# Three small copies of v off the DMA queue, and one clear moved, in a sliding-window attention with an MLP behind it

## The chip, the cores and the metric

The kernel runs on one core of one Trainium2 chip. A core has a matrix engine (TensorE, PE in the profile), VectorE (DVE), ScalarE (ACT), GpSimd (POOL) and SyncE (SP), each with its own queue of instructions, worked off in order, and sixteen DMA engines. DMAs are issued from SyncE's and GpSimd's queues here. The metric is the device time of one execution in microseconds (us).

## The reference

Attention with a causal window of 64 over 8 batches of 8 heads, 576 rows and 64 dimensions, and an MLP over the 4608 rows that come out, with the gate h * cos(h):

```python
scores = scale * np.matmul(q, k.transpose(0, 1, 3, 2))
rel = pos[:, None] - pos[None, :]
mask = (rel >= 0) & (rel < window)          # window = 64
scores = np.where(mask, scores, -1000000000.0)
attn = np.exp(scores - np.max(scores, axis=-1, keepdims=True))
attn = attn / (np.sum(attn, axis=-1, keepdims=True) + 1e-09)
x = np.matmul(attn, v)                      # then (B, S, H * D) -> 4608 x 512
h = x @ w_in                                # w_in 512 x 2048
g = h * np.cos(h)
out = g @ w_out                             # w_out 2048 x 512
```

## The kernel before

The MLP goes in nine tiles of 512 rows. Two heads make a pair; a unit is (batch b, pair p, block j) of 64 query rows, with 128 keys and both heads of the pair on the 128 partitions. Units are worked in groups of three or four. A group n goes through these steps:

- scores on TensorE (`s`, `Gs`), then mask and maximum on VectorE (`m`, `Gm`), the exponentials on ScalarE (`e`, `Ge`, L318), the reciprocal of their sums on VectorE (`i`, `Gi`, L325),
- the product of both, on GpSimd or VectorE (`n`, `Gn`, L332; the last letter names the engine, p for GpSimd, d for VectorE),
- the transpose of the product: for some groups on TensorE with a copy behind it (`w`, `Gw`, then `c`, `Gp`), for the others as a DMA transpose from SyncE's queue (`Gc`, L344).

Then come the values, that is weights times v, on TensorE (`v` for half of tile 0, `V` for pair p of tile 1), and a copy into xT (`x`, `X`). The MLP of a tile is `h` (first matrix), the sine on ScalarE (`S`), the gate on VectorE (`g`), `o` (second matrix) and `oc` (the copy of its result). An `h` takes one of five PSUM banks and needs the gate done that last used it.

v is loaded in chunks of 128 rows (`Lv0`, `Lv1` for batches 0 and 1) into every second slot of a tile of v. A unit whose keys begin in the middle of a chunk takes the slots between, which hold the neighbouring halves of two chunks. `spread_v` (L186 to L194) fills these slots with a copy from one slot into the next, by half of the partitions: as a DMA from SyncE's queue (letter s), on VectorE (d) or on GpSimd (p). Its steps are zA, zB and zC for batch 0 and y for batch 1; y.0 is the first half, y.1 the second. Both halves of a pair are needed before the values that use them: zB before v.0.1, y before V.0.

`ms.4` to `ms.7` clear the q blocks that batch 3 will use.

For tile 0 and the start of tile 1 the order of all instructions is written out by hand in the string FIRST: a step's place in it is its place in the queue of its engine. From there on a planner puts the attention of the next batches between the matrix products of a tile by due times (`at`, `pump`). For batch 2 it issues the transposes of k (`turn_k`, L247) and two copies of v on SyncE; for later batches the copies of v are on GpSimd.

The loads of weights, q, k and v go through GpSimd's queue: `Lwi` and `Lwo` for the four parts of w_in and w_out, `Lq` and `Lk` for q and k. 

Of the kernel before, what the change touches and what calls it, by code (L numbers as in the profile page):

```python
# [10 lines left out]
def _safe_warn(msg, *a, **kw):  # L11
# [58 lines left out]
)  # L70


# [1 line left out]
def kernel(  # L74
# [10 lines left out]
    B, H, S, D = q.shape  # L85
# [45 lines left out]
    def copy(engine, out, in_):  # L131
        {"a": nc.scalar.copy, "p": nc.gpsimd.tensor_copy}.get(engine, nc.vector.tensor_copy)(out, in_)  # L132
# [54 lines left out]
    def spread_v(b, half, engine="p", lo=0, hi=4):  # L187
        vt = vtiles[b % 2]
        hi = min(hi, 4 - (half == 0))
        d = slice(64 * half, 64 * half + 64)  # L190
        of = 2 * lo + 2 * (half == 0)
        to, of = vt[d, 2 * lo + 1:2 * hi:2], vt[d, of:of + 2 * (hi - lo) - 1:2]
        if engine == "s":
            nc.sync.dma_start(out=to, in_=of)  # L194
        else:
            copy(engine, to, of)
# [27 lines left out]
    def put_q(b, p, engine=None):  # L224
        of, to = in_order(st.pop(("tq", b, p)), qtiles[b * PAIRS + p], b)
        if b:
            copy(engine, to, of)
        elif engine == "a":
            nc.scalar.mul(to, of, scale)
        else:  # L230
            nc.vector.tensor_scalar(to, of, scale, None, ALU.mult)
# [17 lines left out]
    def put_k(b, p, engine="a"):  # L249
        kt = k_tile(b)[:, p]  # L250
        of, to = in_order(st.pop(("tk", b, p)), kt, b)
        copy(engine, to, of)
# [16 lines left out]
    def g_scores(n, which):  # L269
        s_ps = bank((BANKS if n < n_listed else S_BANKS)[which], "s_ps")  # L270
        units = groups[n]
        s_ps = s_ps[:, 0:len(units) * 128].rearrange("p (u c) -> p u c", c=128)
        if n < n_first:
            m0 = 2 if units[0][2] else 0
            for h in range(2):
                d = slice(64 * h, 64 * h + 64)
                nc.tensor.matmul(out=s_ps[d].rearrange("p u c -> p (u c)"), lhsT=ident[d, d],
                                 rhs=mask16[d, m0:m0 + len(units)].rearrange("p u c -> p (u c)"),
                                 start=True, stop=False, skip_group_check=True)
        for u, (b, p, j) in enumerate(units):  # L280
            kt = st["kT", b, p]
            lo = max(64 * j - 64, 0)
            rhs = kt[:, lo:lo + 128].rearrange("d (a t) -> d a t", a=2)
            if j and j % 2 == 0:
                rhs = rhs[:, ::-1, :]
            if b > 1:
                nc.tensor.matmul(out=s_ps[:, u].rearrange("p (a t) -> p a t", a=2),  # L287
                                 lhsT=qblocks[(b % 2) * PAIRS + p][:, j].rearrange("d h t -> d (h t)"), rhs=rhs,
                                 start=True, stop=True, skip_group_check=True)
                continue  # L290
            for h in range(2):
                d = slice(64 * h, 64 * h + 64)
                nc.tensor.matmul(out=s_ps[d, u].rearrange("p (a t) -> p a t", a=2),  # L293
                                 lhsT=qtiles[b * PAIRS + p][d, 64 * j:64 * j + 64], rhs=rhs[d], start=n >= n_first,
                                 stop=n >= n_first or u == len(units) - 1, skip_group_check=True)
        st["s", n] = s_ps


    def g_max(n):
        s_ps, units = st["s", n], groups[n]  # L300
        negm = att.tile([128, GF], F32, tag="negm", name="negm", bufs=8)
        if n < n_first:
            nc.vector.tensor_reduce(out=negm[:, 0:len(units)], in_=s_ps, op=ALU.max, axis=AX.X, negate=True)
        else:
            s = att.tile([128, GF, 128], F32, tag="s", name="s", bufs=4)
            for u, (b, p, j) in enumerate(units):
                nc.vector.tensor_tensor_reduce(out=s[:, u], in0=s_ps[:, u], in1=mask[:, 2 - j % 2 if j else 0],  # L307
                                               scale=-scale if b else -1.0, scalar=BIG, op0=ALU.add, op1=ALU.min,
                                               accum_out=negm[:, u:u + 1])
            st["s", n] = s  # L310
        st["m", n] = negm
# [152 lines left out]
    n = n_listed  # L464
# [45 lines left out]
    def spread_first(lo, hi):  # L510
        return lambda i, engine: spread_v(0, i, engine, lo, hi)
# [10 lines left out]
             "pq": lambda p, engine: put_q(0, p, engine), "pk": lambda p, engine: put_k(0, p, engine),  # L522
             "Pq": lambda p, engine: put_q(1, p, engine), "Pk": lambda p, engine: put_k(1, p, engine),
             "zA": spread_first(0, 1), "zB": spread_first(1, 3), "zC": lambda engine: spread_v(0, 1, engine, 3, 4),
             "y": lambda half_, engine: spread_v(1, half_, engine),
             "s": lambda p, g, which: g_scores(2 * p + g, which), "m": lambda p, g: g_max(2 * p + g),
             "e": lambda p, g: g_exp(2 * p + g), "i": lambda p, g: g_inv(2 * p + g),
# [12 lines left out]
    for mt in range(1, n_mt):  # L540
# [5 lines left out]
        for ff in range(n_ff):  # L546
# [8 lines left out]
            e = ff % 2  # L555
# [5 lines left out]
        for ms0 in range(0, MT // 128, 2):  # L561
            o_sb = moe.tile([128, 2, d_model], F32, tag="out", name="out_sb", bufs=OUTS)
            o_ps = [bank(which, "out_ps") for which in (("O1",) if mt == n_mt - 1 and ms0 else ("O1", "O0"))]
            for e in range(2):
                ms = ms0 + e
# [44 lines left out]
```

## Time and profile before

| | |
|---|---|
| median of 3 runs | 313.28 us (312.45 to 314.71) |
| the profiled execution | 313.61 us, span 311.8 us |
| granted TensorE clock | 1.0 |
| busy in the span | PE 95%, ACT 76%, DVE 74%, POOL 61% |
| the chain that ended last | PE 83%, DMA 8%, ACT 3%, POOL 3% |
| v copies by DMA in the first 60 us | issued at 17.35, 18.11, 19.49 and 47.60 us |
| tile 0 and the start of tile 1 | until about 64 us |

The span is the stretch between the first and the last instruction of one profiled execution; the time of the execution holds some 1.8 us more. The profile's views name instructions by engine, line, operation and tiles, with output before input. In views in order of time the first number is the start within the span and the second the duration, both in us; several instructions of a kind that follow each other are merged into one row (x3), and what stands in brackets is the idle time of the engine ahead of the row and what ended it. SPq is SyncE's queue of DMA issues: the duration there is that of issuing, and the data land later. PEld is TensorE's loading of weights.

### The profile page before, as it was taken

To read this page: it belongs to the slowest core of one execution; us is meant where nothing else is said; L and a number is where in the kernel's file an instruction comes from. 1 tells how busy PE (TensorE), PEld (TensorE's weight loads), DVE (VectorE), ACT (ScalarE), POOL (GpSimd) and SP (SyncE) were. 2 spreads that over 40 slices of the span, in tenths; PEclk is the share of its full clock that TensorE was granted. 3 is DMA by queue.
4 is the path that set the end of the run, shared out by engine and by line. 5 is a ranking of instruction groups with operands and counts; after the bars stand their busy time and mean duration, and the time that the engine had idled before them with its cause. 6 is when DMAs were issued, how large, how long until landed. Compare 5 with 4: busy or idle time off the path is not lost.

```text
span 311.8 us, 7954 instructions
## 1 busy us (share of the span) xinstructions
PE 296.8 (95%) x2627; PEld 161.6 (52%) x2659; DVE 230.6 (74%) x877; ACT 236.1 (76%) x785; POOL 191.7 (61%) x227
## 2 busy tenths in 40 slices
PE   3789999799999999999999999999999999999996
PEld 3667844445555455445545545455545554454443
DVE  5898978489777976798579867987698758335801
ACT  5998799486997799769976997699869986116600
POOL 8988576993569678966997699769902850000000
PEclk9999999999999999999999999999999999999999
DMA  7999999999959996999999998999794333011011
GB/s 150 175 212 187 200 178 132 132 162 167 241 82 113 138 235 84 117 116 230 120 105 129 216 138 94 139 230 120 91 135 155 65 80 141 0 69 68 0 67 70
DMA packets 155162, 41.17 MB, mean 132 GB/s; under 512 B 143280, under 2 KB 150384, under 8 KB 155120
## 3 DMA queue, kind: packets, MB, share of 16 engines
q0 software_dynamic: 100192, 18.06, 80.8%
q1 hardware_dynamic: 54784, 22.40, 38.1%
q8 instruction: 21, 0.34, 0.5%
q14 instruction: 21, 0.17, 0.2%
q10 hardware_dynamic: 144, 0.20, 0.2%
HBM read 36.70 MB, written 9.44 MB: 148 GB/s over the span
## 4 chain that ended last, share of the span: by engine, by line
PE 83%; DMA 8%; ACT 3%; POOL 3%; DVE 1%; issue 1%; SPq 1%; POOLq 0%; DVEq 0%; ACTq 0%
PE h_ps L428 34%; PE out_ps L570 34%; DMA w_in<-in_moe_w_in_dram 4%; PE s_ps L287 4%; PE h_ps L392 3%; PE o_ps L359 3%; ACT e L318 2%; PE tq_ps L214 2%; DMA wT<-w 2%; DMA k<-in_k_dram 2%; POOL v L183 1%; PE out_ps L440 1%; PE out_ps L411 1%; DVE s L307 1%; SPq L344 1%
## 5 line engine op out<-in xcount | busy, mean ns | idle before, releaser
L570 PE MATMUL out_ps<-w_out,gT 128*128 128x512 bf16 x482 | 116.1, 379 | 0.8 <-issue 0.2
L428 PE MATMUL h_ps<-xT,w_in 128*128 128x512 bf16 x498 | 115.2, 379 | 1.0
L556 ACT ACTIVATE sin<-h_ps 128x512 f32<-128x512 f32 x128 | 74.0, 598 | 34.0 <-PE h_ps L428 30.8
L318 ACT ACTIVATE e<-s,negm 128x128 f32<-128x128 f32 x256 | 98.7, 388 | 0.7 <-DVE negm L307 0.6
L559 DVE TENSOR_TENSOR gT<-h_ps,sin 128x512 bf16<-128x512 f32 x128 | 81.6, 685 | 21.4 <-ACT sin L556 20.6
L332 POOL TENSOR_TENSOR w<-e,rden 128x512 bf16<-128x512 f32 (+1 forms) x75 | 71.2, 965 | 38.7 <-DVE rden L325 36.9
L428 PEld LDWEIGHTS <-w_in 128*128 128x128 bf16 x512 | 48.6, 98 | 53.9 <-issue 0.4
L570 PEld LDWEIGHTS <-gT 128*128 128x128 bf16 x496 | 45.9, 98 | 44.2
L307 DVE CUSTOM_DVE_ANT_0 s<-s_ps,mask 128x128 f32<-128x128 f32 x256 | 58.5, 286 | 1.2 <-PE s_ps L293 1.0
L318 ACT ACTIVATION_READ_ACCUMULATOR e<-s,negm 128x1 f32 x256 | 48.1, 188 | 0.0
L177 POOL DMA_DIRECT2D q<-in_q_dram x36 | 29.0, 805 | 11.1 <-DMA v<-in_v_dram 4.3
L183 POOL DMA_DIRECT2D v<-in_v_dram x40 | 34.1, 873 | 0.4 <-DMA q<-in_q_dram 0.3
L177 POOL DMA_DIRECT2D k<-in_k_dram x36 | 28.8, 802 | 6.9 <-DMA k<-in_k_dram 5.6
L325 DVE RECIPROCAL rden<-den 128x4 f32<-128x4 f32 (+1 forms) x79 | 13.7, 173 | 21.0 <-ACT e L318 17.2
L132 ACT COPY out_sb<-out_ps 128x512 f32<-128x512 f32 (+1 forms) x18 | 10.2, 565 | 24.5 <-PE out_ps L570 18.4
L287 PEld LDWEIGHTS <-qB 128*128 128x128 bf16 x216 | 17.1, 98 | 14.2
L132 DVE CAST xT<-o_ps 128x512 bf16<-128x512 f32 x24 | 15.6, 677 | 10.8 <-PE o_ps L359 10.8
L132 DVE COPY out_sb<-out_ps 128x512 f32<-128x512 f32 x18 | 12.4, 689 | 13.5 <-PE out_ps L570 12.4
L132 DVE COPY qB<-tq_ps 64x576 bf16<-64x576 bf16 x48 | 21.6, 450 | 0.3
L287 PE MATMUL s_ps<-kT,qB 128*128 128x128 bf16 x216 | 21.9, 219 | 0.0
L307 DVE DVE_READ_ACCUMULATOR2_ANT negm<- 128x1 f32 x256 | 21.3, 83 | 0.0
L132 POOL COPY v<-v 64x1536 bf16<-64x1536 bf16 (+1 forms) x10 | 16.8, 1676 | 0.3
(64 smaller groups left out, 253.2 us busy)
## 6 DMA issues: line engine op xcount, KB each, us to landing
out_dram<-out_sb SPq DMA_DIRECT2D x16, 512.0 KB, 7.8
v<-in_v_dram POOLq DMA_DIRECT2D x32, 128.0 KB, 6.1
q<-in_q_dram POOLq DMA_DIRECT2D x36, 96.0 KB, 8.9
k<-in_k_dram POOLq DMA_DIRECT2D x36, 96.0 KB, 9.0
w_in<-in_moe_w_in_dram POOLq DMA_DIRECT2D x4, 512.0 KB, 9.2
w_out<-in_moe_w_out_dram POOLq DMA_DIRECT2D x4, 512.0 KB, 11.3
wT<-w SPq DMA_TRANSPOSE x68, 4.1
q<-in_q_dram POOLq DMA_DIRECT2D x7, 144.0 KB, 6.2
```

The costliest lines, as they stand in the source:

```text
L132: {"a": nc.scalar.copy, "p": nc.gpsimd.tensor_copy}.get(engine, nc.vector.tensor_copy)(out, in_)
L177: nc.gpsimd.dma_start(out=st[name, b][:, c].rearrange("p (h d) -> p h d", h=H), in_=src.rearrange("h p d -> p h d"))
L183: nc.gpsimd.dma_start(out=vt.rearrange("p (h d) -> p h d", h=H), in_=v[b, :, c * 128:c * 128 + n, :].rearrange("h p d -> p h d"))
L287: nc.tensor.matmul(out=s_ps[:, u].rearrange("p (a t) -> p a t", a=2), lhsT=qblocks[(b % 2) * PAIRS + p][:, j].rearrange("d h t -> d (h t)" ...
L307: nc.vector.tensor_tensor_reduce(out=s[:, u], in0=s_ps[:, u], in1=mask[:, 2 - j % 2 if j else 0], scale=-scale if b else -1.0, scalar=BIG, ...
L318: nc.scalar.activation(e[:, u], s[:, u], AF.Exp, bias=negm[:, u:u + 1], scale=1.0 if n < n_first else -1.0, accum_out=den[:, u:u + 1])
L325: nc.vector.reciprocal(out=rden[:, 0:len(groups[n])], in_=den[:, 0:len(groups[n])])
L332: (nc.gpsimd if engine == "p" else nc.vector).tensor_tensor(out=w[:, 0:u], in0=e[:, 0:u], op=ALU.mult, in1=rden[:, 0:u].unsqueeze(2).to_br ...
L428: nc.tensor.matmul(out=st["h", ff], lhsT=w_in_sb[:, ks, ff * 128:ff * 128 + 128], rhs=st["xT", mt][:, ks], start=start, stop=stop)
L556: nc.scalar.activation(sin, h_ps, AF.Sin, bias=math.pi / 2.0)
L559: nc.vector.tensor_tensor(out=gt[:, e], in0=h_ps, in1=sin, op=ALU.mult)
L570: nc.tensor.matmul(out=o_ps[e], lhsT=gT[ff // 2][:, ff % 2, ms * 128:ms * 128 + 128], rhs=w_out_sb[:, ff], start=ff == 0, stop=ff == n_ff - 1)
```

## The change

The DMAs zB.0.s and zB.1.s (64 partitions, two slots of 512) and zC.s (one slot) become copies on VectorE, each at a later place of FIRST than the DMA had: zB.0.d behind the maximum m.3.1, zB.1.d behind the copy c.0.1.d, zC.d behind the gate g.1.0. The clear ms.4.d moves from behind e.3.1 to behind g.0.3, ahead of ms.6. The DMA y.0.s (three slots) becomes two copies on GpSimd: yA.p (two slots) behind the product Gn.14.p, and yB.p (one slot) behind Gn.13.p. The copy y.1.d of the other half stays on VectorE. SyncE's queue has four DMAs fewer and nothing new; TensorE's and ScalarE's orders are the same.

The diff, cut to the lines of FIRST in which these steps stand:

```diff
-    "e.2.1 zB.0.s zB.1.s n.0.1.p i.1.1 w.3.0 v.0.0 c.3.0.d x.0.0.a s.3.1.3 Gm.10 v.1.0 m.3.1 i.2.1 "
-    "Gs.11.2 Gm.9 Gm.12 n.1.1.p x.1.0.a e.3.1 ms.4.d w.0.1 w.1.1 c.1.1.a i.3.1 h.0.0.1 h.0.1.4 tb "
-    "n.2.1.p c.0.1.d Lwi.3 w.2.1 h.0.2.0 n.3.1.p v.0.1 S.0.0 Gm.11 w.3.1 S.0.1 h.0.3.3 Lwo.0 S.0.2 "
-    "c.2.1.d c.3.1.d v.1.1 zC.s g.0.0 S.0.3 h.0.4.2 ms.5.d x.0.1.a x.1.1.d h.0.5.1 g.0.1 h.1.0.4 g.0.2 "
-    "g.0.3 S.0.4 ms.6.d h.0.6.0 h.1.1.3 S.0.5 S.1.0 Lq1.2 S.0.6 g.0.4 S.1.1 g.1.0 h.1.2.2 Lk1.2 ms.7.d "
...
-    "Gi.14 Gm.15 Gs.17.1 oc.1.d Gc.9 y.0.s Gn.11.p Gi.13 Gm.16 o.1.2 Ge.8 Ge.16 Ge.15 y.1.d Gn.14.p Gi.8 "
-    "Gc.12 Gm.17 o.0.3.0 Gi.16 Gn.13.p Gc.11 Gn.8.p Lq2.3 Lq2.4 Lq2.5 o.2.2 Gn.16.d Gw.8 Gc.14 Gc.13 "
...
+    "e.2.1 n.0.1.p i.1.1 w.3.0 v.0.0 c.3.0.d x.0.0.a s.3.1.3 Gm.10 v.1.0 m.3.1 zB.0.d i.2.1 Gs.11.2 Gm.9 "
+    "Gm.12 n.1.1.p x.1.0.a e.3.1 w.0.1 w.1.1 c.1.1.a i.3.1 h.0.0.1 h.0.1.4 tb n.2.1.p c.0.1.d zB.1.d "
+    "Lwi.3 w.2.1 h.0.2.0 n.3.1.p v.0.1 S.0.0 Gm.11 w.3.1 S.0.1 h.0.3.3 Lwo.0 S.0.2 c.2.1.d c.3.1.d v.1.1 "
+    "g.0.0 S.0.3 h.0.4.2 ms.5.d x.0.1.a x.1.1.d h.0.5.1 g.0.1 h.1.0.4 g.0.2 g.0.3 ms.4.d S.0.4 ms.6.d "
+    "h.0.6.0 h.1.1.3 S.0.5 S.1.0 Lq1.2 S.0.6 g.0.4 S.1.1 g.1.0 zC.d h.1.2.2 Lk1.2 ms.7.d Lq1.3 h.0.7.4 "
...
+    "Gs.17.1 oc.1.d Gc.9 Gn.11.p Gi.13 Gm.16 o.1.2 Ge.8 Ge.16 Ge.15 y.1.d Gn.14.p yA.p Gi.8 Gc.12 Gm.17 "
+    "o.0.3.0 Gi.16 Gn.13.p yB.p Gc.11 Gn.8.p Lq2.3 Lq2.4 Lq2.5 o.2.2 Gn.16.d Gw.8 Gc.14 Gc.13 Lk2.0 "
...
              "zA": spread_first(0, 1), "zB": spread_first(1, 3), "zC": lambda engine: spread_v(0, 1, engine, 3, 4),
+             "yA": lambda engine: spread_v(1, 0, engine, 0, 2), "yB": lambda engine: spread_v(1, 0, engine, 2, 3),
              "y": lambda half_, engine: spread_v(1, half_, engine),
```

16 rows, old and new, of the table FIRST are left out of this document.

## The prediction

> **What bounds the kernel now.** I read first the page's engine shares and the slices over the span, then the chain that ended last, then the order of time on SyncE, GpSimd and VectorE in the first 60 us.
>
> ```profile
> PE 296.8 (95%) x2627; PEld 161.6 (52%) x2659; DVE 230.6 (74%) x877; ACT 236.1 (76%) x785; POOL 191.7 (61%) x227
> PE   3789999799999999999999999999999999999996
> PE 83%; DMA 8%; ACT 3%; POOL 3%; DVE 1%; issue 1%; SPq 1%; POOLq 0%; DVEq 0%; ACTq 0%
> ```
>
> TensorE is busy 95% of the span, and from the second tile on (64 us) nearly without a gap: of 92 to 124 us it is busy 31.77 of 32.00. The change leaves TensorE's instructions and their order alone, so it can only move the date at which that steady part begins. What is to be won or lost lies in the first 64 us, where the chain leaves TensorE twice for a transfer. The second time is the one that matters (chain, start and us):
>
> ```profile
> 49.20 1.05 POOL w L332
> 50.25 0.59 SPq L344
> 50.93 1.21 SPq L344
> 52.22 5.68 DMA wT<-w
> 57.95 0.66 PE o_ps L359 x30
> ```
>
> Read backwards: at 57.95 TensorE starts V.2, the values of pair 2 in tile 1. It had finished V.1 at 56.49 and waited 1.46 us for the transposed weights of group 13 (step Gc.13). GpSimd had multiplied them by 50.24 (Gn.13), but SyncE issued their transpose only at 52.22, because its queue was late. Why it was late stands in SyncE's own order of time and in its waits:
>
> ```profile
> 43.78 2.58 SPq L344 DMA_TRANSPOSE wT<-w  x2
> 47.60 0.60 SPq L194 DMA_DIRECT2D v<-v  x1
> 48.30 3.83 SPq L344 DMA_TRANSPOSE wT<-w  x3
> SPq L194 <- DMA v<-in_v_dram: 16.8, 2, 15.7
> ```
>
> The two transposes Gc.10 and Gc.9 are out at 46.36. Then the queue stands before y.0.s, the copy of the first half of batch 1's v, until the loads of that v have landed (47.55); y.0.s takes its 0.60, and Gc.12, Gc.11 and Gc.14 follow at 48.30, 49.62 and 50.93, each 1.22 long, all of them on weights that had been ready (GpSimd ended Gn.12 at 45.52, Gn.11 at 46.52, Gn.14 at 48.21). Gc.13 comes behind them at 52.22.
>
> **The change, part by part.**
>
> *y.0.s off SyncE.* Gc.12 can go at 46.40, Gc.11 at 47.70, Gc.14 at 49.00 (three steps of 1.30), Gc.13 at 50.30, when Gn.13 has just ended. That is 1.9 us earlier. How long a transpose then takes to land is bounded by this tile's rows:
>
> ```profile
> DMA to landing us min/median/max: 3.8/5.5/6.7
> ```
>
> So the weights land between 54.1 and 57.0, with the median 55.8; I take the 5.69 of Gc.13 itself: 56.0, before V.1 ends. TensorE gains the whole 1.46 us; at the worst latency still 0.9.
>
> *yA and yB on GpSimd.* Here are the three multiplications between which they stand, and what GpSimd takes for such copies later in the run:
>
> ```profile
> 47.38 0.83 POOL L332 TENSOR_TENSOR w<-e,rden 128x384 bf16<-128x384 f32 x1 [0.86 <-PE s_ps L293]
> 49.20 1.04 POOL L332 TENSOR_TENSOR w<-e,rden 128x512 bf16<-128x512 f32 x1 [0.99 <-DVE rden L325]
> 51.14 1.04 POOL L332 TENSOR_TENSOR w<-e,rden 128x512 bf16<-128x512 f32 x1 [0.90 <-DVE rden L325]
> L132 POOL COPY v<-v 64x2048 bf16<-64x2048 bf16 x5 | 9.5, 1894 | 0.3
> L132 POOL COPY v<-v 64x1536 bf16<-64x1536 bf16 x5 | 7.3, 1458 | 0.0
> ```
>
> 512 columns more cost 436 ns, so yA (64x1024) is 1458 - 436 = 1.02 us and yB (64x512) 0.59. yA falls into the idle 0.99 before Gn.13, yB into the idle 0.90 before Gn.8: both are covered, to within 0.03. Without that cover Gn.13 would end up to 1.0 later; Gc.13 would then land by 57.0, and TensorE would still gain. Behind yB it is tighter, for Gn.8 is waited for: TensorE stood 0.59 us before Gw.8 at 52.23, and everything from there to V.2 follows without a gap.
>
> *Copies on VectorE and GpSimd at once.* The rows of the v copies that VectorE makes already:
>
> ```profile
> 17.56 0.25 DVE L132 COPY v<-v 64x512 bf16<-64x512 bf16 x1
> 18.57 0.34 DVE L132 COPY v<-v 64x512 bf16<-64x512 bf16 x1
> 49.69 1.09 DVE L132 COPY v<-v 64x2048 bf16<-64x2048 bf16 x1
> ```
>
> The first met an idle GpSimd, the other two a multiplication (until 18.76 and 50.24). If the last one waited out the 0.55 us that the multiplication still had, its own work was 0.55, and 512 columns cost about (0.55 - 0.25) / 3 = 0.10. By this reading y.1.d (49.69, in VectorE's queue ahead of Gi.8, which Gn.8 needs) and yB now meet. If the copy goes first, yB runs from 50.79 to 51.38, and Gn.8 starts 0.26 late; if yB goes first, Gi.8 is late by yB's 0.59. If the two engines do not block each other it costs nothing. Bounds 0 and 0.59; I take 0.3, near the first order, since the copy has been waiting by then. The Trainium skill speaks against the change here: by "SBUF — State Buffer", section "Who interferes with whom", a VectorE copy in a two-port mode and a GpSimd instruction take one port pair by turns, and the later of them is blocked until the other ends. By that rule this term is 0.26 to 0.59 and never 0; the three rows fit it.
>
> *zB on VectorE, ms.4 later.* zB.0.d and zB.1.d are 64x1024: 0.35 free, up to 1.4 if one waits for a whole multiplication of 1.04. zB.0.d (after m.3.1, at 21.03) finds GpSimd idle from 20.81; i.2.1, Gm.9 and Gm.12 behind it move by 0.3, and since ms.4 (0.45 from start to start) has left, i.3.1 is 0.2 early. zB.1.d then starts at 23.34, and n.3.1 on GpSimd at about 23.37: a tie. If VectorE is first, its delay is swallowed by its idle 0.67 us before c.3.1.d (25.45). If GpSimd is first, zB.1.d ends at 24.75. v.0.1, which now starts at 24.61 (right after the old zB.1.s landed, 24.55), would start at 24.8, c.3.1.d ends 0.4 later, and VectorE enters the gates 0.4 late.
>
> In the gates ms.4 and zC.d (0.25) come back into the queue, between g.0.3 and g.0.5: 0.7 us. Cover: TensorE takes 0.87 us for each h, VectorE 0.6 for each g, and h waits only for the g five banks back. h.1.3 (32.95) needs g.0.5, which now ends at 32.31: cover 0.64. With 0.7 and a VectorE that is 0.2 early TensorE waits hardly; with VectorE 0.4 late it waits some 0.4, and h.1.7 ends 0.55 late.
>
> *Three fewer transfers early.* zB.0.s, zB.1.s and zC.s (320 KB, issued from 17.35 on) share the sixteen DMA engines with the weight loads. At the rate of that stretch (about 200 GB/s) they are 1.6 us of transfer; I take 1.0 for the loads behind them. Two of these are waited for:
>
> ```profile
> 26.84 3.34 PE L392 MATMUL h_ps<-xT,w_in 128*128 128x256 bf16 x29 [0.18 <-DMA w_in<-in_moe_w_in_dram]
> 45.04 1.89 PE L411 MATMUL out_ps<-w_out,gT 128*128 128x512 bf16 x8 [0.30 <-DMA w_out<-in_moe_w_out_dram]
> ```
>
> The first wait, and the gap before v.0.1, give at most 0.45, which VectorE's gates then take back in part; the end of the gates lies between 0.2 early and 0.55 late, and I take 0.15 late. The second gives 0.3, whatever came before.
>
> **Sum.** Gates +0.15, w_out -0.3, yB +0.3, V.2 -1.46: -1.3 us. The profiled execution took 313.61 (span 311.8 and 1.8 around it), which becomes 312.3; the median of the runs, 313.28, lies 0.33 lower, so I forecast 312.0. All good ends: -0.2 - 0.3 + 0 - 1.46 = -2.0 (311.3). All bad ends: +0.55 - 0.3 + 0.59 - 0.9 = -0.1 (313.2). The likeliest case by itself: 311.3 to 313.2.
>
> **Rivals.**
>
> 1. *Taken back at the second tile's scores* (chance 0.2). The third kT transpose of batch 2 lands at 74.53, and the first scores that need it start at 75.13: 0.6 us. SyncE issues it earlier if TensorE is earlier, but GpSimd's loads, which fill the DMA engines there (7.5 us from issue to landing), keep their dates. If the landing stays, only 0.6 is kept: 312.7. For it speaks the DMA load; against it, that the issue at 67.00 follows Gc.18, which moves with TensorE.
>
> 2. *Slower: VectorE becomes the bound of the gates* (0.15). Place: zB.0.d to g.0.5. If both zB copies wait for a whole multiplication, VectorE is 2 x 1.4 = 2.8 behind, less its idle 0.67, plus zC.d 0.25: 2.4, of which the banks cover about 0.4 to 0.6. TensorE then loses about 2 us, and as the exponentials start only after the last sine, all behind moves. Above 1.76 (1.46 + 0.3) it decides: about 0.3 to 1.0 slower, 313.9. Against it: GpSimd is idle when zB.0.d starts.
>
> 3. *More is freed* (0.15). If the loads gain the full 1.6 us, VectorE wins the tie and nothing meets at yB, the freed waits reach 2.4 us: 310.9.
>
> 4. *SyncE's queue doesn't move the landing* (0.05). If transposes land only when the loads ahead have drained, V.2 still waits: 313.2.
>
> **How the numbers follow.** The forecast has 0.45. No more than 2 in 10 is to lie outside, so the range takes in rivals 1, 3 and 4 and most of 2: 310.5 to 314.6. Faster or slower by 1% (3.1 us, about what a measurement of this kernel can tell from no change) would need more than all the waits of the first 64 us that the change reaches, or a VectorE 5 us late in the gates. No case above gives either; I leave 0.06 for the far end of rival 3 and 0.08 for that of rival 2, whose price rests on three rows, and 0.86 between.
>
> **What would show it.** Right: Gc.12 issued near 46.4 and Gc.13 near 50.4, no wait before V.2, and steady tiles that start 1 to 1.5 us earlier. yB ending after 51.1, with Gn.8 late, shows the meeting with y.1.d; a zB.1.d longer than 1 us shows the lost tie. Wrong: if V.2 still waits for wT, if h.1.2 or h.1.3 waits over 1 us for a bank, or if tile 2's first scores wait for kT.

## The result, and the profile after

| | before | after |
|---|---|---|
| median of 22 runs each | 313.01 us (311.44 to 315.28) | 314.07 us (313.18 to 316.93) |
| ratio after to before | | 1.0052, 95% interval 1.0036 to 1.0068 |
| the profiled execution | 313.61 us, span 311.8 | 313.24 us, span 311.5 |

Slower by half a per cent (1.06 us between the medians; the ratio, 0.52%, is 1.6 us); forecast was 1.3 us faster. The two profiled executions say the opposite of the medians: that of after is one of its fastest, that of before one of its slower ones. A single pair of spans would have misled here. What can be compared between executions are the stages: the date at which TensorE starts the same weight load in each. Those dates carry the rest of this text; a difference of them is called the lead (negative is earlier than in the profile shown of before).

The page of after, in the lines that answer to those shown of before (engine shares, TensorE's slices, the chain):

```profile
PE 297.3 (95%) x2627; PEld 161.6 (52%) x2659; DVE 232.8 (75%) x880; ACT 236.2 (76%) x785; POOL 193.5 (62%) x229
PE   3889999999999999999999999999999999999995
PE 84%; DVE 7%; POOL 2%; DMA 2%; issue 2%; ACT 2%; SPq 0%; DVEq 0%; POOLq 0%; ACTq 0%
```

The chain has changed its character: transfers fell from 8% to 2%, VectorE rose from 1% to 7%. What was removed is gone, and VectorE took its place. First what came as predicted, SyncE's queue and TensorE between 53 and 59 us, in order of time (start, us, what):

```profile
43.81 8.12 SPq L344 DMA_TRANSPOSE wT<-w  x6
```

```profile
55.01 0.44 PE L359 MATMUL o_ps<-wT,v 128*64 128x64 bf16 x16
55.38 0.40 PE L341 MATMUL tw_ps<-ident,w 128*128 128x128 bf16 x4
55.61 1.03 PE L411 MATMUL out_ps<-w_out,gT 128*128 128x512 bf16 x4
56.57 0.95 PE L359 MATMUL o_ps<-wT,v 128*64 128x64 bf16 x48
```

Six transposes go out without the pause that y.0.s made, Gc.13 among them at 50.74 instead of 52.22, and V.1, V.2 and V.3 (48 products from 56.57) run through: the wait of 1.46 us is gone. Gc.13 also landed sooner than its earlier issue alone explains: 2.46 us behind its issue (53.20), where it took 5.68 and 5.35 in the two profiles of before. In those GpSimd issues its first load of q 0.1 us ahead of Gc.13 or 0.3 behind it; in every other profile here that load goes out at least 1.1 us behind, and Gc.13 takes 2.4 to 3.6. No run changes that distance alone, so that the loads of q lengthen it is likely but not shown.

Then the gates. First VectorE in the kernel before, between the gates g.0.3 and g.0.5:

```profile
29.48 0.54 DVE L508 MEMSET qB<- 128x576 uint32 x1
29.93 1.22 DVE L404 TENSOR_TENSOR gT<-h_ps,sin 128x512 bf16<-128x512 f32 x2
31.23 0.54 DVE L508 MEMSET qB<- 128x576 uint32 x1
31.68 3.68 DVE L404 TENSOR_TENSOR gT<-h_ps,sin 128x512 bf16<-128x512 f32 x6
```

After, VectorE, then GpSimd, then TensorE from 20 to 34 us:

```profile
20.76 0.41 DVE L132 COPY v<-v 64x1024 bf16<-64x1024 bf16 x1
...
23.13 1.36 DVE L132 COPY v<-v 64x1024 bf16<-64x1024 bf16 x1
...
29.73 1.15 DVE L508 MEMSET qB<- 128x576 uint32 x2
30.79 1.22 DVE L404 TENSOR_TENSOR gT<-h_ps,sin 128x512 bf16<-128x512 f32 x2
32.05 0.29 DVE L132 COPY v<-v 64x512 bf16<-64x512 bf16 x1
32.51 0.54 DVE L508 MEMSET qB<- 128x576 uint32 x1 [0.17 <-issue]
33.06 4.88 DVE L404 TENSOR_TENSOR gT<-h_ps,sin 128x512 bf16<-128x512 f32 x8
```

```profile
23.14 1.06 POOL L332 TENSOR_TENSOR w<-e,rden 128x512 bf16<-128x512 f32 x1
```

```profile
26.50 6.89 PE L392 MATMUL h_ps<-xT,w_in 128*128 128x256 bf16 x56
33.80 4.53 PE L392 MATMUL h_ps<-xT,w_in 128*128 128x256 bf16 x40 [0.42 <-DVE gT L404]
```

zB.0.d found GpSimd idle and took 0.41; zB.1.d, by the profile, began 0.01 us ahead of the product n.3.1 on GpSimd and took 1.36: it ended 0.29 us behind that product (24.49 and 24.20). g.0.5, which started at 31.68 before, starts at 33.06, and TensorE waits for it at 33.80. Last, a place that the prediction doesn't mention, the values near 123 us, first in the kernel before, where nothing waits, then after:

```profile
122.88 1.20 PE L359 MATMUL o_ps<-wT,v 128*64 128x64 bf16 x64
```

```profile
121.78 0.89 PE L359 MATMUL o_ps<-wT,v 128*64 128x64 bf16 x44
123.03 0.55 PE L359 MATMUL o_ps<-wT,v 128*64 128x64 bf16 x20 [0.36 <-DMA wT<-w]
```

The lead of TensorE, by the same weight load in each trace. The columns are the dates of that load in the profile shown of before, the values are differences in us, and a step between two columns is what was won or lost there:

| at | 26.9 | 37.4 | 54.4 | 57.9 | 90 | 95 | 122 | 125 | 305 |
|---|---|---|---|---|---|---|---|---|---|
| after | -0.34 | +0.84 | +0.55 | -1.10 | -1.09 | -1.09 | -1.09 | -0.58 | -0.57 |

So the gates lose 1.18, the wait for w_out at 45 us that before has and after has not brings 0.36, V.2 brings 1.65, and 0.51 more go at 123 us.

### The profile page after: what moved, and what is told of

It is laid out like the page before. It is cut to its first block, busy times and chain, and to the rows that moved or that the text cites. A ratio compares the mean times of both kernels' runs of the same rounds, so it can differ in the third digit from the quotient of the medians.

```text
span 311.5 us, 7948 instructions
## 1 busy us (share of the span) xinstructions
PE 297.3 (95%) x2627; PEld 161.6 (52%) x2659; DVE 232.8 (75%) x880; ACT 236.2 (76%) x785; POOL 193.5 (62%) x229
## 4 chain that ended last, share of the span: by engine, by line
PE 84%; DVE 7%; POOL 2%; DMA 2%; issue 2%; ACT 2%; SPq 0%; DVEq 0%; POOLq 0%; ACTq 0%
PE h_ps L428 34%; PE out_ps L571 31%; PE s_ps L287 4%; PE out_ps L411 3%; PE o_ps L359 3%; PE tq_ps L214 2%; DVE s L307 2%; PE h_ps L392 1%; DVE gT L404 1%; PE s_ps L293 1%; DVE v L132 1%; PE out_ps L440 1%; POOL w L332 1%; POOL v L132 1%; PE tk_ps L211 1%
## 5 line engine op out<-in xcount | busy, mean ns | idle before, releaser
L132 POOL COPY v<-v 64x1536 bf16<-64x1536 bf16 (+3 forms) x12 | 18.8, 1570 | 0.3
```

## The experiments

All of them keep the reference's computation. "y part" means y.0.s as yA.p and yB.p; "z part" means zB and zC on VectorE and ms.4 moved. Each was timed in five rounds beside the kernel before, whose medians on the chips used were 312.38, 312.83, 312.62 and 312.75 us.

### Both kernels once more, and each part alone

The edits: none; none; and one part of the change each.

```diff
# y_only: the y part on the kernel before
-Gc.9 y.0.s Gn.11.p ... Gn.14.p Gi.8 ... Gn.13.p Gc.11
+Gc.9 Gn.11.p ... Gn.14.p yA.p Gi.8 ... Gn.13.p yB.p Gc.11
# z_only: the changed kernel with y.0.s back
-Gc.9 Gn.11.p ... Gn.14.p yA.p Gi.8 ... Gn.13.p yB.p Gc.11
+Gc.9 y.0.s Gn.11.p ... Gn.14.p Gi.8 ... Gn.13.p Gc.11
```

> The changed kernel once more, unchanged, for a second profile: the one in hand had a span 0.3 us shorter than before's while the median of its runs is 1.06 us longer, so it may not be a typical execution. Theory A (the lead of the steady part carries to the end, and what is lost is lost in the gates): span about 0.3 to 1.1 us above the first profile's 311.5, and the difference stands already at the start of the steady part (first long row of L428 behind the sine at 63.6 in the first profile). Theory B (the lead at 64 us is given back in the later tiles, where weights land just in time): the steady part starts at 63.6 again, and the time is lost in waits of o_ps for wT near 123 us and at the same place of later tiles. Theory C (the matrix engine is granted less clock): the long matmul rows themselves are slower, and the runs' clocks lie below 1.

> The kernel before, unchanged, for a second profile and for the clock of its runs. Ratio 1.000 by every theory. Theory A and B: the steady part starts at 64.7 again, or somewhat earlier, as the median (313.01) lies 0.6 below the profiled execution; no wait of o_ps for wT near 123 us. Theory C: its runs show a clock of 1.000 throughout, while those of the changed kernel go down to 0.989.

> Only the y part: y.0.s replaced by yA and yB on GpSimd; zB, zC as DMAs and ms.4 as before. Theory A: V.2 no longer waits (1.46 us), yB's meeting with y.1.d costs 0.56 as in the changed kernel, nothing is lost in the gates: 0.9 to 1.4 us faster than before (ratio 0.996 to 0.997). Theory B: the lead is given back near 123 us: within 0.4 us of before. Theory C: slower than its lead says by the clock.

> Only the z part: zB.0.d, zB.1.d, zC.d on VectorE and ms.4 behind g.0.3, with y.0.s as a DMA as before. Theories A and B: the gates end about 0.84 us late (h.1.7 at 38.3 in place of 37.5), less the 0.3 us wait for w_out that goes: 0.5 to 1.0 us slower than before (ratio 1.002 to 1.003). By B the changed kernel should be as slow as this one, by A about 1 us faster than it.

Measured: after again 313.83 us, ratio 1.0047 (1.0020 to 1.0075); before again 312.48, 0.9992 (0.9967 to 1.0017); the y part 311.84, 0.9993 (0.9965 to 1.0020); the z part 314.10, 1.0045 (1.0023 to 1.0067). The lead:

| at | 26.9 | 37.4 | 54.4 | 57.9 | 90 | 95 | 122 | 125 |
|---|---|---|---|---|---|---|---|---|
| after again | -0.16 | +1.02 | +0.74 | -0.91 | -0.90 | -0.90 | -0.90 | -0.35 |
| before again | +0.40 | +0.40 | +0.05 | -0.73 | -0.73 | -0.73 | -0.73 | -0.73 |
| y part alone | -0.20 | -0.20 | -0.48 | -2.14 | -2.13 | -2.12 | -2.12 | -2.12 |
| z part alone | +0.58 | +1.76 | +1.40 | -0.25 | -0.25 | +0.50 | +0.50 | +1.07 |

The loss belongs to the z part alone: 1.18 us in the gates, each time it is there, and then at 95 and 125 us. The y part keeps its gain to the end. More follows. In the z part alone V.2 brings 1.65 as well, with y.0.s still in SyncE's queue: Gc.13 goes out at 52.38 there and lands at 55.51, before TensorE asks for it. The dates of the first 27 us differ by up to 0.9 us between executions, in the kernel before too (0.40 here). The 0.36 at w_out come in the kernel before as well when run again, so they are no effect of the change. And the wait that the y part removes is not always 1.46: in the second profile of before it is 0.67:

```profile
57.22 0.66 PE L359 MATMUL o_ps<-wT,v 128*64 128x64 bf16 x30 [0.67 <-DMA wT<-w]
```

Theory A and theory B both had part of it: the gates lose, and something is given back in later tiles. C, the granted clock, fell: it was 0.998 to 1.0 in these profiles. Executions with 0.995 or less are longer (median 312.94 against 312.13 us in the 35 of the kernel before timed here), but they are 12 of those 35 and only 2 of the 12 of after again.

### What the gates lose: zB.1.d, or ms.4 and zC.d

```diff
# zb_clear: zB.1.d where GpSimd issues a DMA and multiplies nothing
-Gm.12 n.1.1.p ... c.0.1.d zB.1.d
+Gm.12 zB.1.d n.1.1.p ... c.0.1.d
# gates_free: ms.4 and zC.d out of the gates
-g.0.3 ms.4.d ... g.1.0 zC.d h.1.2.2 ... Pk.3.d Lv0.4 ... Gi.11 oc.0.d
+g.0.3 ... g.1.0 h.1.2.2 ... Pk.3.d zC.d Lv0.4 ... Gi.11 ms.4.d oc.0.d
# mended: both, and yB.p behind Gn.8.p
-Gn.13.p yB.p Gc.11 Gn.8.p
+Gn.13.p Gc.11 Gn.8.p yB.p
```

> The changed kernel with zB.1.d put behind the maximum Gm.12, where GpSimd issues a DMA and multiplies nothing. Theory A (three things add up in VectorE's queue: zB.1.d blocked, +0.26 us at the first gate; ms.4, +0.60; zC.d, +0.52; about 0.5 of it covered): zB.1.d takes about 0.4 us instead of 1.36, the first gate starts at about 25.7, and TensorE loses 0.8 to 1.0 us between 26.9 and 37.4 us instead of 1.18; the time is 0.2 to 0.4 us below the changed kernel's. Rival (the lost tie costs it all): the loss falls below 0.3 us, the time by about 1 us.

> The changed kernel with zC.d behind Pk.3.d and ms.4.d behind Gi.11, both out of the gates; zB.1.d stays where it is blocked. Theory A: g.0.4 and g.0.5 start 0.6 and 1.1 us earlier, and TensorE loses 0 to 0.3 us between 26.9 and 37.4 us instead of 1.18; the time falls by 0.8 to 1.1 us, to that of the kernel before or a little under it. Rival (the lost tie costs it all): 0.9 us of the loss stay.

> The changed kernel with both mends and yB.p behind Gn.8.p. Theory A: no loss in the gates, Gn.8 at about 50.6 and not blocked, TensorE 1.8 to 2.4 us ahead of the kernel before (its first profile) at 64 us. Theory D (a transpose that overlaps the 8 KB fetch of instructions near 121 us lands 0.7 us later than its neighbours; the three more instructions of VectorE have moved the fetch one transpose ahead, onto one that TensorE waits for): 0.4 to 0.6 us are lost again near 123 us, as VectorE's instructions are as many as in the changed kernel; time 0 to 0.8 us under the kernel before. Rival to D (the wait near 123 us comes from a late start out of the gates): no wait there, 1.0 to 1.5 us under the kernel before.

Measured: zb_clear 313.99 us, ratio 1.0056 (1.0025 to 1.0088); gates_free 313.14, 1.0020 (1.0003 to 1.0038); mended 313.84, 1.0043 (1.0022 to 1.0064). The stretch from 26.9 to 37.4 us falls into three stops, each at its own product of `h` (loss in us; zB.1.d's duration beside it):

| | zB.1.d | 28 us: first gate late | 29.4 us: last part of w_in | 31 to 34 us: ms.4, zC.d |
|---|---|---|---|---|
| after | 1.36 | 0.28 | 0.22 | 0.68 |
| after again, z part alone | blocked | 0.28, 0.28 | 0 | 0.90, 0.90 |
| zb_clear | 0.61 | 0 | 0 | 0.83 |
| gates_free | blocked | 0.28 | 0.47 | 0 |
| mended | 0.61 | 0 | 0 | 0 |

Theory A is shown, and its rival (the lost tie costs it all) fell: the tie is worth 0.28, the two instructions put among the gates 0.7 to 0.9. ("Blocked" is 1.37 us, in each of these three profiles.) TensorE stops at the same place in zb_clear as in after:

```profile
34.54 4.53 PE L392 MATMUL h_ps<-xT,w_in 128*128 128x256 bf16 x40 [0.42 <-DVE gT L404]
```

In gates_free that wait is gone, but TensorE waits longer than in after for the last part of w_in, which landed at 30.59 here:

```profile
30.63 7.60 PE L392 MATMUL h_ps<-xT,w_in 128*128 128x256 bf16 x68 [0.30 <-DMA w_in<-in_moe_w_in_dram]
```

The last quarter of w_in lands between 27.9 and 30.6 us in these traces, in after at 29.57 (29.39 before), though three transfers fewer are ahead of it. The medians did not follow the gates, though: zb_clear was no faster than after, and mended, with no loss in the gates and a lead of 2.04 us at 64 us, lost 1.56 at 91 us and 0.62 at 123. That is the second half of the cause.

### The waits at 91 and 123 us

The clue is in the trace's DMA records: near 121 us a single 8 KB transfer of the kind "instruction", a fetch of instructions, goes over the DMA engines (queue q14; in the window from 120 to 124 us of after, with packets, MB and share of the 16 engines):

```profile
q1 hardware_dynamic: 1544, 0.37, 55.1%
q14 instruction: 1, 0.01, 0.7%
```

The fetch starts at 121.03. The transpose issued at 119.94 takes 3.05 us to land, where its neighbours take 2.35 and 2.45. In the kernel before the fetch meets the transpose behind that one (3.13 us), and TensorE waits for nothing. y_plus3 adds three tiny clears to the y part alone, in an idle place of VectorE:

```diff
+def extra_clears(n):
+    for _ in range(n):
+        nc.vector.memset(extra, 0.0)      # 128x1, read by nobody
-Gn.17.d X.1.d
+Gn.17.d dm.3 X.1.d
```

> The kernel before with the y part alone and three clears of one number per partition on VectorE, behind Gn.17.d (about 57 us), that nothing reads. Theory D: as with the y part alone until 120 us, then the sixth transpose of the tile takes over 3.0 us to land and TensorE waits 0.3 to 0.6 us near 121 to 123 us; the time is 0.3 to 0.6 us above the y part alone (311.8). Rival (the wait belongs to the copies of zB and zC or the dates they bring): no wait there, 311.8 us.

Measured: 312.39 us, ratio 0.9997 (0.9975 to 1.0019). TensorE at 122 us:

```profile
121.09 0.89 PE L359 MATMUL o_ps<-wT,v 128*64 128x64 bf16 x44
122.39 0.55 PE L359 MATMUL o_ps<-wT,v 128*64 128x64 bf16 x20 [0.41 <-DMA wT<-w]
```

The wait is there, 0.57 us of lead are lost, the fetch comes 1.1 us earlier in the tile (120.4 instead of 121.1, with TensorE 0.3 later), and the transpose that it meets takes 3.12 us. Nothing of the z part is in this kernel.

The next four were to tell what sets the wait at 91 us, and to move the fetch away from 123:

```diff
# mended_yb: mended with yB.p back
-Gn.13.p Gc.11 Gn.8.p yB.p
+Gn.13.p yB.p Gc.11 Gn.8.p
# mended_dm: mended_yb and four clears
-Gn.17.d X.1.d
+Gn.17.d dm.4 X.1.d
# y_late: y part alone, yB.p behind Gn.8.p;  y_only_2: y part alone again
```

> The kernel of the run mended with yB.p back behind Gn.13.p. Theory E (the 1.23 us that TensorE waited for wT at 91 us in that run come from yB.p behind Gn.8.p, which sends out GpSimd's loads of batches 2 and 3 about 0.9 us later, so that the last lands at 87.4 us and the transposes behind them at 90 to 91): the last k load of the stretch lands at 85.5 us or earlier, TensorE waits under 0.2 us at 91 us; no loss in the gates, 0.5 to 0.6 us lost near 123 us (theory D). Time 1.0 to 1.5 us below the run mended. Rival (any start out of the gates that is 2 us early meets the loads there): 0.8 us or more are lost at 91 us again.

> mended_yb with four clears of one number per partition on VectorE behind Gn.17.d (about 57 us), which nothing reads. Theory D: the 8 KB fetch comes about 1.3 us earlier near 121 us and meets the transpose before, for which there is some 0.7 us of room: TensorE waits under 0.15 us between 121 and 125 us, and the time is 0.4 to 0.6 us below mended_yb. Rival (it is the number of transposes or their dates, not the fetch): the wait of 0.4 to 0.5 us stays.

> The kernel before with the y part alone, yB.p behind Gn.8.p instead of Gn.13.p. Theory E: yB.p takes about 0.6 us, Gn.8 is not blocked, TensorE is at 57.9 us where it is with the y part alone (V.2 waits for the landing of Gc.13 either way), but GpSimd's loads go out 0.5 to 0.9 us later, the last k load lands at 86 to 87.5 us, and TensorE waits 0.5 to 1.3 us at about 91 us: time 0.5 to 1.3 us above the y part alone. Rival (yB's place is harmless): no wait there, the time of the y part alone.

> The y part alone once more, for its time and for a second profile. Theory: V.2 waits under 0.2 us for wT, no wait near 123 us, and the time is 0 to 1.0 us below the kernel before; if the gain at V.2 is of size 0.7 instead of 1.6 us, this second profile shows the dates of Gc.13's landing in the two kernels that close together.

Measured: mended_yb 312.92 us, ratio 0.9999 (0.9971 to 1.0027); mended_dm 313.50, 1.0018 (0.9981 to 1.0054); y_late 313.78, 1.0032 (0.9995 to 1.0069); y_only_2 311.80, 0.9971 (0.9939 to 1.0003).

Theory E (GpSimd's loads set the wait at 91 us) fell as the cause in general: in mended_dm the last k load landed at 83.65 us, earlier than in y_only (84.30), which waits for nothing there, and TensorE waited 1.27; in y_late it landed at 86.6 and TensorE waited for nothing there. In mended itself that load landed later than in any other run, at 87.37, so there it may have had a part. Nor did mended_dm move the wait near 123 us: four clears on top of the three z copies left the fetch where it was. The gates of mended_yb lost 1.19, not to VectorE but to w_in's last part, which landed at 30.27:

```profile
30.32 7.92 PE L392 MATMUL h_ps<-xT,w_in 128*128 128x256 bf16 x71 [1.01 <-DMA w_in<-in_moe_w_in_dram]
```

y_late's profiled execution is its fastest (span 310.7, lead -1.16 at the end, no wait at 91 or 123), so what its slower ones lose isn't seen. Six of its twelve had a granted clock of 0.995 or less (median 314.50 us), but the other six, with 313.05, do not show the lead of the trace either; that stays open.

What remained was VectorE's number of instructions. y_plus7 adds to it alone; the other two kernels make VectorE's program shorter by putting the clears ms.4 to ms.7 on GpSimd:

```diff
# y_plus7: y part alone and seven clears
+Gn.17.d dm.7 X.1.d
# y_clears: y part alone; clears_p: mended_yb; both with
-ms.4.d, ms.5.d, ms.6.d, ms.7.d
+ms.4.p ms.5.p Lwo.3 ... Lv1.3 ms.6.p ms.7.p
```

> The y part alone with seven clears of one number per partition on VectorE behind Gn.17.d, instead of three. Theory D2 (each VectorE instruction added brings the 8 KB fetches that follow VectorE's count forward; the one that lies at 93.4 us in the kernel before then comes together with the other one at about 91 us, and the transpose between them lands 1.2 to 1.6 us late): TensorE waits 1.0 to 1.4 us for wT at about 90 us, as in the runs mended and mended_dm, and 0.4 to 0.5 near 121 to 123; time 1.2 to 1.8 us above the y part alone. Rival (it was the copies of zB and zC, or the loads): no wait at 90 us, 0.57 us at most lost near 122.

> mended_yb with the clears ms.4 to ms.7 on GpSimd, two ahead of Lwo.3 and two behind Lv1.3, where GpSimd waits in the kernel before. VectorE has one instruction fewer than the kernel before instead of three more. Theory D2: the fetches are back where they were, and TensorE waits neither at 91 nor near 123 us. In the gates nothing is lost to VectorE; the last part of w_in may cost 0 to 1.0 us. Time 1.0 to 2.0 us below the changed kernel, 0 to 1.0 below the kernel before. Rival (the waits belong to the z copies): 0.5 us lost near 123 us as in the changed kernel.

> The kernel before with the y part alone and the clears ms.4 to ms.7 on GpSimd at those places; VectorE has four instructions fewer than the kernel before. Theory D2: no wait for wT at 91 or near 123 us, the lead of about 2.1 us at 64 us is kept to the end; time 0 to 0.5 us below the y part alone (311.8) if GpSimd's idle time covers the clears. Rival (GpSimd is not idle there): Lwo.3 or the loads behind Lv1.3 go out later, and TensorE waits for w_out near 45 us or for k near 75 us: up to 1 us above the y part alone.

Measured: y_plus7 313.33 us, ratio 1.0014 (0.9987 to 1.0040); clears_p 312.28, 0.9984 (0.9961 to 1.0006); y_clears 312.73, 0.9994 (0.9967 to 1.0020). TensorE in y_plus7 at 91 us:

```profile
89.30 0.89 PE L359 MATMUL o_ps<-wT,v 128*64 128x64 bf16 x44
91.46 0.51 PE L359 MATMUL o_ps<-wT,v 128*64 128x64 bf16 x20 [1.28 <-DMA wT<-w]
```

All traces together, in the order of VectorE's instructions against the kernel before. The dates of the fetches are those of the trace less the lead, so they stand against the same tile; another 8 KB fetch lies at 90.8 to 91.4 in all of them (92.0 in mended):

| kernel | VectorE instructions | 2nd fetch near 91 us | fetch near 123 us | lost at 90 to 95 | lost at 122 to 125 |
|---|---|---|---|---|---|
| y_clears | -4 | 93.7 | 124.8 | 0 | 0 |
| clears_p | -1 | 93.4 | 123.3 | 0 | 0 |
| before, before again | 0 | 93.4 | 123.5, 123.8 | 0 | 0 |
| y_only, y_only_2, y_late | 0 | 93.4 | 123.3 | 0 | 0 |
| y_plus3 | +3 | 92.8 | 122.2 | 0 | 0.57 |
| after, after again, zb_clear, gates_free, mended_yb | +3 | 92.5 to 92.7 | 122.1 | 0 | 0.51 to 0.58 |
| z_only | +3 | 92.2 | 122.1 | 0.75 | 0.57 |
| mended | +3 | 92.4 | 122.2 | 1.56 | 0.62 |
| mended_dm | +7 | 91.4 | 122.2 | 1.38 | 0.58 |
| y_plus7 | +7 | 91.1 | 122.0 | 1.39 | 0.21 |

So the rival "it is the copies, or the loads" fell. With no more instructions than before, no kernel loses at either place, with the z part (clears_p) or without; with three more all lose near 123 us; with seven more the two fetches near 91 us come together, and the transpose that both overlap takes 4.06 us in y_plus7, 2.45 in y_only. z_only and mended lose at that place with three more only. In z_only the first of the two fetches starts 2.05 us behind the issue of the transpose, which takes 3.41 us; where nothing is lost, that distance is 2.16 to 2.45 and the transpose takes 2.43 to 2.59. In mended both fetches and a third, of 16 KB, fall into the transpose (4.22 us). What moved these fetches in z_only and mended was not tested. Nor was a fetch moved without a change of the program: that it is the fetch that delays the transpose rests on the dates, which agree in all 17 traces. That the fetch near 123 goes no further with seven than with three is not explained. clears_p has the whole change mended and stands at 0.9984, the y part alone at 0.9993 and 0.9971: none of these is shown faster than the kernel before, and the lowest medians are those of the y part alone. The waits are read in single profiles; the times of these kernels differ too little for most of the ratios to tell them apart.

## Why the prediction was wrong

The direction failed, at two steps.

*"Gates +0.15" is the term that was mis-sized: 1.18 us.* The tie between zB.1.d and n.3.1 was named, and its loss stands in the bad end alone (+0.55 for all of the gates); GpSimd won, as the 1.36 us show. That agrees with the Trainium skill, "SBUF — State Buffer", section "Who interferes with whom", where the later of two such instructions is blocked until the other ends; which was the later, 0.01 us in the profile can't tell. But that is the smaller piece, 0.28. The larger: ms.4 was put at 0.45 and zC.d at 0.25, by their rows in other surroundings. Between the gates they cost 0.60 (g.0.3 to g.0.4 grew from 1.21 to 1.81 us) and 0.52 (g.1.0 to g.0.5 from 1.20 to 1.72). With an entry 0.26 late, g.0.5 came 1.38 us late, and not 0.5 or 1.1 as by the two cases of the prediction. The cover was sized right: TensorE started 0.34 early, so VectorE was 1.72 late against it, and 1.18 were lost, which leaves 0.54 of the 0.64 predicted. Rival 2 named the place, with another mechanism (two blocked copies); one was blocked, and its condition, over 1.76 us, was not reached. That its 313.9 lies near the measured 314.07 is luck.

*The sum ended at 64 us.* That the change "leaves TensorE's instructions and their order alone, so it can only move the date at which that steady part begins", is false here: 0.5 us more went at 123 us, because three more instructions on VectorE move an instruction fetch onto a transpose that had only 0.3 us of room (it took some 0.65 longer to land than its neighbours, and TensorE waited 0.36). Nothing in the prediction looked for it.

*What was right.* Off SyncE: Gc.12 at 46.44, Gc.14 at 49.04 and Gc.13 at 50.74 (50.30 predicted), no wait before V.2. The landing came at 53.20 and not at 56.0: the 5.69 us taken from Gc.13's own row measured 2.46, an error that cost the forecast nothing, as V.1 ends later than both. yA took 1.03 (1.02 predicted). yB met y.1.d, as was thought possible: it took 1.07 and not 0.59, ending 0.46 behind y.1.d. But TensorE lost only 0.08 there (0.3 predicted, and 0.26 or 0.59 by the two orders; the first is 0.24 by its own rows), since Gn.8 waited for y.1.d and Gi.8 anyway. w_out's 0.3 came (0.36), though not from the change. Rival 1 fell: the lead is the same at 57.9 and 90 us. Rival 4 fell with the wait at V.2. The freed transfers did what rival 3 hoped for the third part of w_in (24.73 instead of 26.79), but nothing for the fourth, and TensorE could not use it.

*"V.2 -1.46" was an upper size.* The wait was 1.46 in one profile of before and 0.67 in the other, and it goes without the y part too: in z_only TensorE reaches V.2 1.4 us later, Gc.13 lands at 55.51 instead of 57.91, and nothing waits. The differences of the medians (y part -0.5 and -0.8 us) fit a wait nearer to the second. Together: gates +1.2, 123 us +0.5, V.2 about -0.7, which is +1.0, against the measured +1.06 us between the medians (the ratio's 1.6 would leave 0.6 unexplained). How the wait is distributed over unprofiled executions was not measured.

## What to carry to other kernels

Price an instruction that goes into an engine's back-to-back stretch by the growth of the step it splits, not by its duration elsewhere, and price a tie as lost. Don't end the sum where the steady part begins: added instructions can move the engine's instruction fetches far behind them, and a DMA transpose with a few tenths of room can be hit. When an effect is under 1%, compare the dates of one and the same instruction in several executions; one pair of spans had the wrong sign here.

## What was not expected of the hardware

- Near 123 us, an 8 KB fetch of instructions that starts 0.9 to 1.5 us behind the issue of a DMA transpose goes with a landing of 2.7 to 3.4 us instead of 2.3 to 2.5, in before (3.13 and 3.36 in its two profiles) as in after (3.05). A transpose whose issue the fetch follows by 2.2 us or more took 2.3 to 2.5. Near 91 us two fetches within 0.5 us of each other went with 4.06 us (y_plus7), 4.05 (mended_dm) and, with a 16 KB fetch besides, 4.22 (mended).
- A copy of 64x512 on GpSimd took 0.94 to 1.07 us (mended, y_late, after), hardly less than 64x1024 (1.03). But VectorE worked beside it each time, and the copy ended 0.46 to 0.47 us behind VectorE's instruction (51.73 and 51.27 in after, 53.55 and 53.08 in y_late), so these rows don't refute the 0.59 of the prediction as its own work.
- Two clears of 128x1152 (bf16) on GpSimd took 2.08 to 2.14 us (clears_p, y_clears), 1.04 to 1.07 each; the same on VectorE 0.54.
